# Weight conversions issued behind the first mixed tokens, and three homes for the bias rows' pieces, in a fused attention and MLP-mixer kernel

## The chip, the cores and the metric

The kernel runs on 1 core of a Trainium2 chip, in one launch. The metric is the device time in microseconds (us) of that core. The kernel before was timed in 3 runs: median 874.73 us, lowest 873.62, highest 876.39. The execution whose profile is shown took 872.61 us; from its first to its last instruction (its span) it took 870.8 us.

The engines are called as the profile calls them: PE is TensorE (matmuls), PEld its weight loads, ACT is ScalarE, DVE is VectorE, POOL is GpSimd, SP is SyncE, which only issues DMAs here. A name with a q behind it (SPq, ACTq) is that engine's instruction queue.

## The reference

Four batches of 576 tokens pass through three blocks. All inputs are float32 except the seven weight matrices of the second and third blocks, which lie in memory as 64-bit floats and are converted on the chip.

```python
# attention: q, k, v of 4 batches x 8 heads x 576 tokens x 64
scores = q @ k^T / 8
cum  = cumsum(max(s, 0))                        # per head, along the tokens
bias = -(cum[:, None] - cum[None, :])
scores = where(causal, -1e9, scores + min(bias, 0))
attn = exp(scores - max) / (sum + 1e-9)
x = (attn @ v), heads side by side               # 4 x 576 x 512

# second block: w_k 512x1024, w_v 1024x512, w_r 512x512
x_prev = x shifted by one token
xk = mu_k * x + (1 - mu_k) * x_prev
xr = mu_r * x + (1 - mu_r) * x_prev
v = max(xk @ w_k, 0)^2 @ w_v
x = sigmoid(xr @ w_r) * v

# third block: a mixer over tokens (w_tok1, w_tok2), then over channels (w_ch1, w_ch2)
```

## The kernel before

Nearly all products are made from two parts, a rounded high part and the rest, so that one product costs three matmuls (function `products`, line 108 in the profile). Every weight block is therefore loaded raw and then converted by `weight_split` (lines 614 to 621): two ACT passes over the block, two DVE passes, one ACT pass that writes the high part, and one subtraction that writes the low part (on POOL for w_k and w_r, on DVE for w_v). The blocks of w_k (8) and w_r (4) are 128 x 512 numbers and have five staging buffers; the 16 blocks of w_v are 128 x 256 and are staged in whatever is free of the six buffers named `xt`. At the start four of those hold the attention's output, so that two are left for w_v.

The program starts with batch 0. Its first 256 tokens of all eight heads come first (`early`, lines 324 to 368 of before): scores on PE, maximum on DVE, exponential on ACT, the row sum on POOL, its reciprocal on DVE, the scaling on POOL, a transpose on PE, a copy T on ACT, and a product with V. Behind each transpose PE runs a few matmuls whose result nobody reads (`keep_busy`, line 162). After each pair of heads `mix` (lines 508 to 517) makes one quarter of the mixed tokens HX: two DVE operations, one on ACT (line 516), one on DVE (line 517). Products with w_k that read HX are called h; they need all four quarters for their last terms. The other mixed tokens of the batch are XR; products with w_r that read them are called r; the products with w_v are called vd and need the squared h, KK. The remaining 320 tokens of batch 0's heads (`late`, lines 392 to 421) run between them.

`split_bias` writes the cumulative sums of s, split in two parts, to DRAM (ext_d) in three pieces of 192 columns. Each piece is put together in one tile e: POOL sets it to ones, DVE writes four of its row groups, ACT's queue issues the store (line 202). The tile e has one buffer, so a piece waits for the store of the piece ahead of it. The late heads load ext_d next to their q and k (`late_load`, tiles X).

The order of all instructions on each engine is fixed when the program is built. A scheduler walks through the operations by priority; `with at(place)` gives the place of what stands inside, smaller places first. Each engine then runs its list strictly in order and waits wherever an operand or a buffer is not ready. DMAs from SP and ACT take eight completion counters in turn; each issue waits until the DMA eight places ahead of it has landed.

Of the kernel before, what the change touches and what calls it, by code (L numbers as in the profile page):

```python
# [9 lines left out]
F32R = mybir.dt.float32r  # L10
# [9 lines left out]
def f32(ap):  # L20
    return ap.bitcast(F32)
# [3 lines left out]
def attention_moe_mixer(  # L25
# [16 lines left out]
    nc = tc.nc  # L42
# [25 lines left out]
    def at(place):  # L68
        return tc.high_priority(tc.cur_priority - int(place * 1000))
# [66 lines left out]
    def pt_tile(slot, dtype=F32):  # L136
        return pt_p.tile([128, (NS - 1) * PW], dtype, tag=f"PT{slot}", name=f"PT{slot}")
# [8 lines left out]
    def constants():  # L146
        nc.gpsimd.affine_select(
            out=maskc[:, 512:640], in_=maskc[:, 512:640], pattern=[[-1, 128]],
            compare_op=ALU.is_ge, fill=-8.0e9, base=0, channel_multiplier=1,
        )  # L150
        make_identity(nc, ident)
        nc.gpsimd.memset(maskp, 0.0)
        nc.gpsimd.tensor_copy(maskp[0:TAIL, S // 2 - TAIL:], maskc[0:TAIL, 512:512 + TAIL])
        nc.scalar.dma_start(out=maskp[TAIL:2 * TAIL, S // 2 - TAIL:], in_=maskc[0:TAIL, 512:512 + TAIL])
# [16 lines left out]
    def bias_rows(cp):  # L171
# [14 lines left out]
                copy("D", e32[:, 1, 0, :], cum[:, a:z], -1.0)  # L186
        return cum, e32

    def split_bias(cp, cum, behind):
        n = 3  # L190
        for c in range(n):
            a, z = S * c // n, S * (c + 1) // n
            e = cp.tile([G, 4, 2, z - a], F32R, name="e")
            if c == 0:
                nc.gpsimd.tensor_copy(f32(e[0:1, 0, 1, 0:1]), behind)
            for r, t in ((1, 1), (3, 1), (0, 0), (2, 0)):
                nc.gpsimd.memset(f32(e[:, r, t, :]), 1.0)
            copy("D", e[:, 0, 1, :], cum[:, a:z])
            nc.vector.tensor_tensor(out=e[:, 2, 1, :], in0=cum[:, a:z], in1=f32(e[:, 0, 1, :]), op=ALU.subtract)
            for x in (0, 2):  # L200
                copy("D", e[:, x + 1, 0, :], f32(e[:, x, 1, :]), -1.0)
            nc.scalar.dma_start(out=ext_d[:, :, :, a:z], in_=f32(e))
# [129 lines left out]
    def early(h, j, V0, cp):  # L332
        x, h0, _ = early_view(h)
        w = 128 * j + 128
        P = cp.tile([128, w], F32, tag=f"E{j}", name=f"P{j}", bufs=2)
        mx = st_p.tile([128, 2], F32, tag="mx", name="mx")
        ps = ps_s.tile([128, 512], F32, tag="s", name="s")
        nc.tensor.matmul(ps[:, 0:w], x[0:D + 2, h - h0, 0, 128 * j:w], x[0:D + 2, h - h0, 1, 0:w], start=True, stop=True)
        softmax_max(j, ps, P, mx, 0, 0, w)
        softmax(j, P, mx, 0)  # L340
        if h == 0 and j == 0:
            with at(2):
                split_bias(cp, cum, P[0:1, 0:1])
        if j == 0:
            pt[0] = ps_t.tile([128, 512], F32, tag="t", name="t")
        ps = pt[0]
        for k in range(j + 1):
            o = 128 * (j + k)
            nc.tensor.transpose(ps[:, o:o + 128], P[:, 128 * k:128 * k + 128], ident)
        keep_busy(4, P, 128)  # L350
        if j == 0:
            return
        T = cp.tile([128, FIRST], F32, tag="T", name="T", bufs=2)
        copy("A", T, ps[:, 0:FIRST])
        if h % 2 == 0:
            early_ps[h // 2] = ps_v.tile([128, QC], F32, tag="v", name="pv")
        pv = early_ps[h // 2]
        r = slice(D * (h % 2), D * (h % 2) + D)
        for k in range(2):
            nc.tensor.matmul(pv[r, 128 * k:QC], V0[:, k, h * D:h * D + D], T[:, QC * k:QC + 128 * k], start=k == 0, stop=k == 1)  # L360
        if h % 2 == 1:
            x = xt[0, h // 2] = xt_p.tile([128, 1 + S], F32, tag="xt", name="xt")
            nc.gpsimd.memset(x[:, 0:1], 0.0)
            copy("D", x[:, 1:1 + QC], pv)
# [136 lines left out]
    def mixed(b, c, i):  # L501
# [3 lines left out]
            return act["HX"].rearrange("p (t k s) -> p t k s", t=2, k=KD)  # L505
        return act[("XK", "XR")[i]]

    def mix(b, c, i, p):
        dst = mixed(b, c, i)
        x = xt[b, p]  # L510
        a, z = CHS[c]
        n = z - a
        t = act["mt"].tile([128, act["mtw"]], F32, tag="t", name="t", bufs=act["mtb"])
        nc.vector.tensor_scalar(out=t[:, 0:n], in0=x[:, 1 + a:1 + z], scalar1=mu[:, i, p:p + 1], scalar2=1.0, op0=ALU.mult, op1=ALU.mult)
        nc.vector.scalar_tensor_tensor(out=t[:, 0:n], in0=x[:, a:z], scalar=omu[:, i, p:p + 1], in1=t[:, 0:n], op0=ALU.mult, op1=ALU.add)
        nc.scalar.activation(out=dst[:, 0, p, 0:n], in_=t[:, 0:n], func=AF.Copy)
        nc.vector.tensor_tensor(out=dst[:, 1, p, 0:n], in0=t[:, 0:n], in1=f32(dst[:, 0, p, 0:n]), op=ALU.subtract)  # L517

    def up(b, c, m):
        n = width(c)  # L520
# [84 lines left out]
    def weight_split(key, hi, lo, half=0, ps=None):  # L605
        t = raw.pop(key)
        low, high = t[:, :, :, 0], t[:, :, :, 1]
        if ps is None:
            copy("A", f32(high), f32(high), 2.0 ** -112)
        else:  # L610
            bank = ps.tile([128, high.shape[1], high.shape[2]], I32, tag="w", name="high")
            copy("A", f32(bank), f32(high), 2.0 ** -112)
            high = bank
        nc.scalar.activation(out=low.bitcast(U32), in_=low.bitcast(U32), func=AF.Copy, scale=TOP3, bias=-0.496)  # L614
        nc.vector.scalar_tensor_tensor(out=low, in0=high, scalar=3, in1=low, op0=ALU.logical_shift_left, op1=ALU.bitwise_or)  # L615
        nc.vector.scalar_tensor_tensor(out=low, in0=high, scalar=-2 ** 31, in1=low, op0=ALU.bitwise_and, op1=ALU.bitwise_or)  # L616
        copy("A", hi, f32(low), 0.5 if half else 1.0)
        if half:
            nc.vector.scalar_tensor_tensor(out=lo, in0=f32(low), scalar=0.5, in1=f32(hi), op0=ALU.mult, op1=ALU.subtract)
        else:  # L620
            nc.gpsimd.tensor_tensor(out=lo, in0=f32(low), in1=f32(hi), op=ALU.subtract)  # L621
# [120 lines left out]

    act["mt"], act["mtb"], act["mtw"] = cp, 1, QC
    constants()
    with at(3):
        mixes()
    for h in range(H):
# [15 lines left out]
    for y, a in enumerate(first):  # L763
        nm, W, sw, f = a
        if y:
            with at(x):
                first_load(*a)
        with at(x + 0.6):
            weight_split((nm, f), W[:, 0, :, f:f + 128], W[:, 1, :, f:f + 128], ps=ps_w if nm == "k" else None)
        x += 1.2  # L770
    cp_s.close()
# [12 lines left out]
    for f in range(0, DM, 128):  # L784
        for k in range(0, KF, 2):
            with at(x):
                weight_load((k, f), rows(w_v, k, k + 2)[:, :, f:f + 128], S // 2, xt_p, "xt")
                weight_split((k, f), wv[:, 0, k:k + 2, f:f + 128], wv[:, 1, k:k + 2, f:f + 128], 1)
            x += 1.5
    todo = {}  # L790
    base = (NS - 2) * H
# [232 lines left out]
```

## Time and profile before

| what | us |
|---|---|
| median of 3 runs (lowest, highest) | 874.73 (873.62, 876.39) |
| the profiled execution | 872.61 |
| its span | 870.8 |
| PE busy, of the span | 840.6 |
| DVE busy | 485.1 |
| ACT busy | 452.6 |
| POOL busy | 343.4 |

Busy time counts PE's matmuls that nobody reads as well. Shares over the whole span say little here, since the start, the middle and the end of the program have different limits; the rows further down are therefore cut by stage.

### The profile page before, as it was taken

To read this page: it belongs to the slowest core of one execution; us is meant where nothing else is said; L and a number is where in the kernel's file an instruction comes from. 1 tells how busy PE (TensorE), PEld (TensorE's weight loads), DVE (VectorE), ACT (ScalarE), POOL (GpSimd) and SP (SyncE) were. 2 spreads that over 40 slices of the span, in tenths; PEclk is the share of its full clock that TensorE was granted. 3 is DMA by queue.
4 is the path that set the end of the run, shared out by engine and by line. 5 is a ranking of instruction groups with operands and counts; after the bars stand their busy time and mean duration, and the time that the engine had idled before them with its cause. 6 is when DMAs were issued, how large, how long until landed. Compare 5 with 4: busy or idle time off the path is not lost. (4 is left out here: it accounts for less than half of the span.)

```text
span 870.8 us, 17455 instructions
## 1 busy us (share of the span) xinstructions
PE 840.6 (97%) x6127; PEld 790.5 (91%) x6127; DVE 485.1 (56%) x1352; ACT 452.6 (52%) x1257; POOL 343.4 (39%) x601
## 2 busy tenths in 40 slices
PE   8889998999899999999999999999999999999998
PEld 5656777988789999999999989999999999999998
DVE  5797776565879566985469757951331222222221
ACT  4688766865886656868377865840310221211210
POOL 4565666864785544645256854720000000000000
PEclk9899999999999999999999999999999999999999
DMA  7943778687974244431234746553021112112100
GB/s 191 266 134 88 199 218 230 192 240 210 252 204 133 70 111 117 100 93 41 83 94 129 230 143 217 177 181 94 7 92 54 44 31 74 42 32 73 38 25 26
DMA packets 88024, 108.36 MB, mean 124 GB/s; under 512 B 11152, under 2 KB 71568, under 8 KB 87936
## 3 DMA queue, kind: packets, MB, share of 16 engines
q1 hardware_dynamic: 81408, 91.56, 37.7%
q0 software_dynamic: 4576, 15.08, 5.5%
q8 instruction: 49, 0.80, 0.4%
q10 hardware_dynamic: 1952, 0.60, 0.3%
q14 instruction: 39, 0.32, 0.1%
HBM read 77.74 MB, written 28.90 MB: 122 GB/s over the span
## 5 line engine op out<-in xcount | busy, mean ns | idle before, releaser
L863 ACT ACTIVATE HID<-c 128x256 fp32r<-128x256 f32 (+1 forms) x96 | 39.3, 410 | 220.9 <-PE c L108 220.8
L108 PE MATMUL vd<-KK,WV 128*128 128x256 f32 (+1 forms) x768 | 120.9, 300 | 0.1
L108 PEld LDWEIGHTS vd<-KK,WV 128*128 128x128 f32 x768 | 106.6, 188 | 2.4 <-issue 0.9
L292 POOL TENSOR_SCALAR P<-P,sum 128x128 f32<-128x128 f32 (+4 forms) x148 | 93.6, 636 | 36.2 <-DVE sum L291 30.2
L108 PE MATMUL h<-XK,WK 128*128 128x320 f32 (+1 forms) x672 | 105.9, 303 | 0.7 <-DVE XK L517 0.5
L108 PE MATMUL c<-HID,WV 128*128 128x256 f32 (+1 forms) x768 | 104.9, 291 | 0.0
L108 PE MATMUL c<-U,WK 128*128 128x256 f32 (+1 forms) x768 | 103.2, 291 | 1.4 <-DVE HID L864 1.4
L289 ACT ACTIVATE P<-P,mx 128x128 f32<-128x128 f32 (+4 forms) x148 | 86.9, 588 | 30.3 <-DVE mx L278 23.0
L108 PEld LDWEIGHTS c<-HID,WV 128*128 128x128 f32 x768 | 100.6, 188 | 0.0
L108 PEld LDWEIGHTS c<-U,WK 128*128 128x128 f32 x768 | 98.6, 188 | 1.7 <-DVE HID L864 1.7
L108 PEld LDWEIGHTS h<-XK,WK 128*128 128x128 f32 x672 | 93.8, 189 | 2.1 <-DVE XK L517 0.7
L864 DVE SCALAR_TENSOR_TENSOR HID<-c,HID 128x256 fp32r<-128x256 f32 (+1 forms) x96 | 43.8, 456 | 81.1 <-ACT HID L863 81.0
L278 DVE CUSTOM_DVE_ANT_0 P<-s,maskc 128x128 f32<-128x128 f32 (+4 forms) x148 | 69.1, 478 | 22.1 <-PE t L435 8.4
L928 DVE TENSOR_TENSOR ut<-c,ut 128x256 f32<-128x256 f32 (+1 forms) x32 | 14.6, 458 | 119.3 <-PE c L108 112.0
L529 POOL TENSOR_TENSOR KK<-k,KK 128x256 fp32r<-128x256 f32 (+1 forms) x64 | 55.8, 877 | 19.8 <-ACT k L528 18.7
L108 PE MATMUL r<-XR,WR 128*128 128x320 f32 (+1 forms) x384 | 60.0, 299 | 0.0
L290 POOL TENSOR_SCALAR sum<-sum 128x1 f32<-128x1 f32 (+1 forms) x148 | 32.4, 219 | 67.6 <-ACT P L289 57.2
L108 PE MATMUL c<-HID,WR 128*128 128x256 f32 (+1 forms) x384 | 54.8, 291 | 0.0
L108 PEld LDWEIGHTS r<-XR,WR 128*128 128x128 f32 x384 | 52.8, 188 | 1.1 <-ACT raw L614 0.4
L108 PE MATMUL c<-U,C1A 128*128 128x256 f32 (+1 forms) x384 | 52.8, 296 | 0.1
L108 PEld LDWEIGHTS c<-U,C1A 128*128 128x128 f32 x384 | 51.5, 190 | 0.3 <-ACT U L913 0.3
L108 PEld LDWEIGHTS c<-HID,WR 128*128 128x128 f32 x384 | 51.3, 188 | 0.0
(133 smaller groups left out, 1658.4 us busy)
## 6 DMA issues: line engine op xcount, KB each, us to landing
X<-hl_d SPq DMA_DIRECT2D x72, 288.0 KB
hl_d<-PB SPq DMA_DIRECT2D x48, 288.0 KB
raw<-in_moe_w_ch_dram POOLq DMA_DIRECT2D x48, 256.0 KB, 3.3
PB<-in_qk_dram SPq DMA_DIRECT2D x48, 144.0 KB
yt<-y_d SPq DMA_DIRECT2D x16, 288.0 KB
u_d<-yt SPq DMA_DIRECT2D x16, 288.0 KB
raw<-in_moe_w_k_dram SPq DMA_DIRECT2D x8, 512.0 KB
raw<-in_moe_w_v_dram SPq DMA_DIRECT2D x16, 256.0 KB
```

The lines of the kernel that those rows point to most:

```text
L108: nc.tensor.matmul(ps, a, b, start=first and i == 0, stop=last and i == n - 1)
L278: nc.vector.tensor_tensor_reduce(out=P[0:m, c0:c1], in0=ps[0:m, 0:c1 - c0], in1=mask[0:m], scale=-scale, scalar=3.0e38 if x == 0 else mx[0 ...
L289: nc.scalar.activation(out=P[0:m, 0:w], in_=P[0:m, 0:w], func=AF.Exp, bias=mx[0:m, x:x + 1], scale=-1.0, accum_out=sm[0:m, 0:1])
L290: nc.gpsimd.tensor_scalar(out=sm[0:m, 0:1], in0=sm[0:m, 0:1], scalar1=1e-9, scalar2=1.0, op0=ALU.add, op1=ALU.mult)
L292: nc.gpsimd.tensor_scalar(out=P[0:m, 0:w], in0=P[0:m, 0:w], scalar1=sm[0:m, 1:2], scalar2=1.0, op0=ALU.mult, op1=ALU.mult)
L529: nc.gpsimd.tensor_tensor(out=kk[:, 1, m, 0:n], in0=t[:, 0:n], in1=f32(kk[:, 0, m, 0:n]), op=ALU.subtract)
L863: nc.scalar.activation(out=hi, in_=ps, func=AF.Relu)
L864: nc.vector.scalar_tensor_tensor(out=lo, in0=ps, scalar=0.0, in1=f32(hi), op0=ALU.max, op1=ALU.subtract)
L928: nc.vector.tensor_tensor(out=t, in0=ps, in1=t, op=ALU.add)
```

## The change

There are two edits.

1. `weight_split` of all four blocks of w_r and of the first four blocks of w_v is placed inside `behind_mix()`. It takes the last ACT and the last DVE operation that `mix` has issued so far, which are those of HX's last quarter, and holds the conversions behind them in the order (`tc.issue_after`). Their loads are not held.
2. The three pieces of the bias rows get a tile each: the two PT tiles, which the late heads use afterwards, and e. All ones are set at the program's start (`bias_ones`), and `split_bias` is placed two places earlier (`at(4)` in place of `at(2)`).

```diff
+    def bias_ones(cp, n):
+        for c in range(n):
+            w = S // n
+            e = pt_tile(c, F32R)[0:G, 0:8 * w] if c < 2 else cp.tile([G, 8 * w], F32R, name="e")
+            e = e.rearrange("g (r t s) -> g r t s", r=4, t=2)
+            for r, t in ((1, 1), (3, 1), (0, 0), (2, 0)):
+                nc.gpsimd.memset(f32(e[:, r, t, :]), 1.0)
+            ones.append(e)
+
+    ones = []
+
     def split_bias(cp, cum, behind):
-        n = 3
+        n = len(ones)
         for c in range(n):
             a, z = S * c // n, S * (c + 1) // n
-            e = cp.tile([G, 4, 2, z - a], F32R, name="e")
-            if c == 0:
-                nc.gpsimd.tensor_copy(f32(e[0:1, 0, 1, 0:1]), behind)
-            for r, t in ((1, 1), (3, 1), (0, 0), (2, 0)):
-                nc.gpsimd.memset(f32(e[:, r, t, :]), 1.0)
+            e = ones[c]
+            nc.gpsimd.tensor_copy(f32(e[0:1, 0, 1, 0:1]), behind)
...
-            with at(2):
+            with at(4):
                 split_bias(cp, cum, P[0:1, 0:1])
...
+    last_mix = {}
+
+    def behind_mix():
+        st = ExitStack()
+        for x in last_mix.values():
+            st.enter_context(tc.issue_after(x))
+        return st
...
-        nc.scalar.activation(out=dst[:, 0, p, 0:n], in_=t[:, 0:n], func=AF.Copy)
-        nc.vector.tensor_tensor(out=dst[:, 1, p, 0:n], in0=t[:, 0:n], in1=f32(dst[:, 0, p, 0:n]), op=ALU.subtract)
+        last_mix[0] = nc.scalar.activation(out=dst[:, 0, p, 0:n], in_=t[:, 0:n], func=AF.Copy).ins
+        last_mix[1] = nc.vector.tensor_tensor(out=dst[:, 1, p, 0:n], in0=t[:, 0:n], in1=f32(dst[:, 0, p, 0:n]), op=ALU.subtract).ins
...
+    bias_ones(cp, 3)
...
-        with at(x + 0.6):
+        with at(x + 0.6), behind_mix() if nm == "r" else ExitStack():
             weight_split((nm, f), W[:, 0, :, f:f + 128], W[:, 1, :, f:f + 128], ps=ps_w if nm == "k" else None)
...
-                weight_split((k, f), wv[:, 0, k:k + 2, f:f + 128], wv[:, 1, k:k + 2, f:f + 128], 1)
+                with behind_mix() if x < 18 + 1.5 * 4 else ExitStack():
+                    weight_split((k, f), wv[:, 0, k:k + 2, f:f + 128], wv[:, 1, k:k + 2, f:f + 128], 1)
```

What this makes of the order, at three places. Line numbers move by up to 18 between the two programs. PE, ACT, DVE and SP issue the same operations as before in another order, POOL two more (the copies of one cell); behind about the 1,670th of PE's 5,970 instructions PE's order is the same again.

The first place is ACT's queue around HX's last quarter (P2 to P4 are exponentials of a late head, high and raw conversion passes, WR and WV the passes that write the high parts). Before:

```order
L75 ACTIVATE raw_661<-raw_661 128x512
L614 ACTIVATE raw_661<-raw_661 128x512
L75 ACTIVATE WR_72<-raw_645 128x4x128
L75 ACTIVATE WR_72<-raw_653 128x4x128
L289 ACTIVATE P4_893,sum_901<-P4_893,mx_894 64x576
L75 ACTIVATE WV_71<-raw_700 128x2x128
L75 ACTIVATE PT0_822<-t_823 128x3x128
L516 ACTIVATE HX_368<-t_544 128x256
L75 ACTIVATE WV_71<-raw_708 128x2x128
L75 ACTIVATE PT0_822<-t_860 128x4x128
L289 ACTIVATE P2_946,sum_951<-P2_946,mx_947 128x384
L75 ACTIVATE WR_72<-raw_661 128x4x128
```

And now:

```order
L532 ACTIVATE HX_370<-t_461 128x256
L75 ACTIVATE T_539<-t_515 128x384
L75 ACTIVATE WK_70<-raw_630 128x4x128
L75 ACTIVATE PT0_824<-t_825 128x3x128
L532 ACTIVATE HX_370<-t_546 128x256
L75 ACTIVATE raw_639<-raw_639 128x512
L630 ACTIVATE raw_639<-raw_639 128x512
L75 ACTIVATE raw_647<-raw_647 128x512
L630 ACTIVATE raw_647<-raw_647 128x512
L75 ACTIVATE raw_655<-raw_655 128x512
L630 ACTIVATE raw_655<-raw_655 128x512
L75 ACTIVATE raw_663<-raw_663 128x512
```

Before, 11 of the 12 passes over w_r and 11 of the 12 over w_v's first four blocks stood ahead of HX's last quarter; now all 24 stand behind it. Behind the last row shown come one more pass over w_r, four over w_v's first two blocks, a copy, an exponential, and then the copy of the first h out of PSUM.

The second place is ACT's queue further on, at w_v's third block, raw_702 (raw_700 before). It is loaded into the buffer of the first, and so after that block's last reader, a DVE operation that follows its WV pass. Before, the WV pass of the first block stood here, and the first pass over raw_700 came sixteen rows behind the last of these:

```order
L75 ACTIVATE T_452<-t_428 128x384
L75 ACTIVATE WV_71<-raw_684 128x2x128
L75 ACTIVATE high_621<-raw_619 128x512
L614 ACTIVATE raw_619<-raw_619 128x512
L75 ACTIVATE WV_71<-raw_692 128x2x128
L289 ACTIVATE P1_520,sum_525<-P1_520,mx_521 128x256
```

Now the two stand two rows apart:

```order
L75 ACTIVATE WR_72<-raw_663 128x4x128
L75 ACTIVATE WV_71<-raw_686 128x2x128
L75 ACTIVATE WV_71<-raw_694 128x2x128
L75 ACTIVATE raw_702<-raw_702 128x256
L630 ACTIVATE raw_702<-raw_702 128x256
L75 ACTIVATE raw_710<-raw_710 128x256
L630 ACTIVATE raw_710<-raw_710 128x256
L543 ACTIVATE KK_682<-k_847 128x256
L543 ACTIVATE KK_682<-k_885 128x256
L532 ACTIVATE XR_681<-t_890 128x256
L75 ACTIVATE WV_71<-raw_702 128x2x128
```

Seven rows behind the last of these stands the copy of the third h (k_935), which frees PE's buffer for the fifth.

The third place is SP's queue, behind the fifth block of w_k. Before:

```order
L371 DMA X0_549<-in_qk_dram 64x1152
L597 DMA raw_610<-in_moe_w_k_dram 128x4x256
L371 DMA X1_552<-in_qk_dram 64x1152
L377 DMA VV0_561<-in_v_dram 128x4x128
L378 DMA VV0_561<-in_v_dram 64x128
L377 DMA VV1_564<-in_v_dram 128x4x128
L371 DMA X2_555<-in_qk_dram 64x1152
```

Now:

```order
L379 DMA X0_551<-in_qk_dram 64x1152
L613 DMA raw_612<-in_moe_w_k_dram 128x4x256
L380 DMA X0_551<-ext_d_73 4x1152
L379 DMA X1_554<-in_qk_dram 64x1152
L380 DMA X1_554<-ext_d_73 4x1152
L385 DMA VV0_563<-in_v_dram 128x4x128
L386 DMA VV0_563<-in_v_dram 64x128
L379 DMA X2_557<-in_qk_dram 64x1152
L380 DMA X2_557<-ext_d_73 4x1152
```

The first load from ext_d, which waits for all three stores, now stands third here; before it stood sixteen issues further back. w_k's seventh block moved ahead of the first two loads of w_v.

## Rows read from the trace of the kernel before

**Rows 1.** Busy us (instructions) of each engine by stage; granted clock, DMA share, GB/s
```profile
0.00:14.60 14.60, 11.04 (x53) 6.58 (x53) 6.41 (x28) 4.61 (x13) 6.07 (x28) 1.00 0.66 149
14.60:34.00 19.40, 16.87 (x105) 13.68 (x105) 14.52 (x48) 11.98 (x32) 9.85 (x24) 0.91 1.06 252
34.00:39.00 5.00, 2.92 (x9) 1.90 (x10) 3.17 (x8) 5.00 (x16) 3.88 (x6) 0.65 1.10 315
...
49.10:63.14 14.04, 12.23 (x62) 7.20 (x60) 13.30 (x30) 12.30 (x28) 10.80 (x9) 1.00 0.30 89
63.14:73.21 10.07, 9.80 (x57) 6.55 (x57) 8.65 (x25) 7.83 (x24) 7.45 (x11) 1.00 0.25 82
73.21:91.82 18.61, 18.61 (x106) 12.20 (x105) 14.51 (x45) 16.20 (x51) 9.18 (x16) 1.00 0.41 113
91.82:140.00 48.18, 48.18 (x305) 36.11 (x304) 32.71 (x97) 31.83 (x93) 31.24 (x55) 1.00 0.74 215
140.00:300.00 160.00, 148.63 (x1061) 139.38 (x1060) 113.41 (x368) 117.03 (x330) 107.46 (x199) 0.99 0.72 197
```

**Rows 2.** PE's instructions in order: start, us, what [idle before, releaser]
```profile
49.10 0.48 PE L108 MATMUL h<-HX,WK 128*128 128x256 f32 x2
...
63.14 0.73 PE L108 MATMUL h<-HX,WK 128*128 128x256 f32 x4 [1.21 <-DVE HX L517]
...
73.21 1.66 PE L108 MATMUL h<-HX,WK 128*128 128x256 f32 x12
...
91.82 1.42 PE L108 MATMUL r<-XR,WR 128*128 128x256 f32 x10
...
147.07 0.30 PE L308 MATMUL s<-X 128*128 128x128 f32 x1 [2.31 <-DMA X<-hl_d]
```

**Rows 3.** Waits up to 70 us: us in total, times, longest
```profile
ACT P L289 <- DVE t L514: 4.0, 1, 4.0
...
POOL e L197 <- DMA ext_d<-e: 4.4, 2, 3.4
```

**Rows 4.** ACT's instructions in order
```profile
18.00 0.56 ACTq L202 DMA_DIRECT2D ext_d<-e  x1
...
32.52 0.56 ACTq L202 DMA_DIRECT2D ext_d<-e  x1
33.12 0.40 ACT L289 ACTIVATE P<-P,mx 128x128 f32<-128x128 f32 x1 [4.00 <-DVE t L514]
...
50.52 0.76 ACT L75 ACTIVATE raw<-raw 128x512 f32<-128x512 f32 x1
51.08 0.77 ACT L614 ACTIVATE raw<-raw 128x512 uint32<-128x512 uint32 x1
...
54.16 0.55 ACT L75 ACTIVATE raw<-raw 128x256 f32<-128x256 f32 x1
54.49 0.55 ACT L614 ACTIVATE raw<-raw 128x256 uint32<-128x256 uint32 x1
...
58.63 0.45 ACT L516 ACTIVATE HX<-t 128x256 fp32r<-128x256 f32 x1
```

**Rows 5.** DVE's instructions in order
```profile
27.05 0.25 DVE L77 CAST e<-st 32x192 fp32r<-32x192 f32 x1 [2.02 <-DMA ext_d<-e]
...
62.67 0.41 DVE L517 TENSOR_TENSOR HX<-t,HX 128x256 fp32r<-128x256 f32 x1
```

**Rows 6.** POOL by form, 49 to 64 us: busy, mean ns of one
```profile
L621 POOL TENSOR_TENSOR WR<-raw,WR 128x512 fp32r<-128x512 f32 x3 | 5.8, 1958 | 1.0 <-ACT WR L75 1.0
...
L621 POOL TENSOR_TENSOR WK<-raw,WK 128x512 fp32r<-128x512 f32 x1 | 1.3, 1302 | 1.4 <-DMA raw<-in_moe_w_v_dram 1.4
```

**Rows 7.** SP's issues in order: a pair of w_v's blocks
```profile
79.76 1.15 SPq L597 DMA_DIRECT2D raw<-in_moe_w_v_dram  x2
```

**Rows 8.** ACT's instructions in order, at that pair's first pass
```profile
82.49 0.44 ACT L75 ACTIVATE raw<-raw 128x256 f32<-128x256 f32 x1 [0.41 <-DMA raw<-in_moe_w_v_dram]
```

## The prediction

> **What bounds the kernel now.** I read the table by stage first, then PE's rows in order, then the rows of the engines that PE waits for. The table [rows 1] is to be read for where PE has time that can be won. From 91.8 us on PE is busy nearly throughout: 48.18 of 48.18 us, then 148.63 of 160, and the rest of the span lies in stages that the change does not touch. So a gain can only come from making PE's dense work start earlier. PE's rows show the points to watch [rows 2]: the first h starts at 49.10, the terms of h that need HX's last quarter start at 63.14 (after 1.21 us idle for DVE line 517), the fifth h starts at 73.21 and the first r at 91.82. From 63.14 on PE has no idle time worth naming up to 140 us; a shift of these points is therefore a shift of the end, as long as the same work is done by then and nothing behind eats it.
>
> HX's last quarter is late because ACT and DVE are full at that time: 12.30 and 13.30 of 14.04 us between 49.10 and 63.14 [rows 1]. ACT writes its share at 58.63 [rows 4] and DVE its share at 62.67 [rows 5]. Ahead of it in their queues stand conversions of w_r and w_v, whose products come 28 us later. Before that the bias rows cost two stalls. POOL waits 4.4 us for stores of ext_d, because the three pieces share a tile [rows 3]. ACT stands still for 4.00 us up to the third store's issue at 32.52 and its next exponential at 33.12 [rows 4]; the wait is put down to DVE's t, which was long done, and the issue itself waits for the DMA eight places ahead of it.
>
> **Edit 2, the bias rows.** The pieces no longer wait for each other. The work is the same but for two copies of one cell; the twelve memsets move to the start, where POOL is busy 6.07 of 14.60 us, and DVE's twelve operations fall into its idle time ahead of the first weight block. I cost them at nothing; without that cover it would be about 0.2 us each. What goes is ACT's 4.0 us and POOL's 4.4 us [rows 3], but they don't add up, since w_k's last blocks are late next. DMA is full from 14.6 to 39 (share 1.06 and 1.10 [rows 1]). The core has moved 149 x 14.6 + 252 x 19.4 = 7.06 MB by 34.0 and 8.64 MB by 39.0. In the new order all that SP and ACT issue up to and including w_k's seventh block is 7.5 MB and up to the eighth 8.85 MB (tile shapes of the code: blocks of 0.52, late q and k 0.29 each, stores 0.59, first heads' data 1.6). At the rates of these rows they land at about 35.3 and 39.8. ACT's queue holds the seventh block's pass ahead of head 5's copy and the eighth's ahead of head 6's, so the last heads can't end before.
>
> Behind the eighth block ACT has five passes of 0.57 us over w_k (0.56 from 50.52 to 51.08 [rows 4]), two copies T and one PT, two exponentials of a late head, and two shares of HX: about 5.5 us. HX's last quarter is then done at about 46 instead of 63.0, with a high end of 50 if chains between engines take as long as they did before.
>
> One row speaks against the change here: the second store, issued at 18.00 [rows 4], held DVE until 27.05 [rows 5], 9 us for a small transfer while SP loads w_k. If the second and third store, now issued together near 16, behave like it, they land near 27, and SP stands in front of the load from ext_d until then. The Trainium skill, "DMA: Bandwidth & Descriptors", section "Issuing engines are not separate DMA queues", says that DMAs of different engines run on the same 16 DMA engines and interleave. This wait agrees with it; by it the stores come no sooner for standing on ACT's queue.
>
> That wait on SP is worth little, by rows: 5.7 MB is issued ahead of it, and the core had moved about that much by 27 (7.06 less 7 us at 252 GB/s is 5.3). The low end is nothing, the high end 3 us on HX's last quarter; I take 1, inside the 46.
>
> **Edit 1, the conversions.** ACT loses ahead of HX's last quarter 11 passes over w_r at 0.57 us and 11 over w_v at 0.33 us (54.16 to 54.49 [rows 4]): 9.9 us. All of it returns behind. Between HX's last quarter and the last share of XR, which r needs, ACT had some 19.5 us of work (7.83 and about 12 of the 16.20 us between 63.14 and 91.82 [rows 1]); now it has 29.4. There the order makes a new stall. w_v's third block is loaded into the first's buffer, and its pass stands two rows behind the second block's WV pass. From the issue of a pair at 79.76 [rows 7] to its first pass at 82.49 [rows 8] it took 2.7 us; with the DVE operation ahead of the issue it makes 3.2 us in which ACT stands, and behind it stand KK, XR and, further on, the copy that frees the buffer for PE's fifth h. So ACT's path is 29.4 + 3.2 = 32.6 us if it is never idle otherwise, and at its share of 12.30 / 14.04 = 88% it is 29.4 / 0.88 + 3.2 = 36.6 us. PE needs for the same stretch, from 63.9 to 91.8, 28 us and so waits for ACT. With the high parts of r's first product behind it, r starts between 46 + 32.6 + 1 = 79.6 and 46 + 36.6 + 1.5 = 84.1; I take 84.5, because PE's own queue adds waits for scores' buffers that DVE frees late. The fifth h would start near 67.
>
> By this r comes 91.8 - 84.5 = 7.3 us earlier. PE is then idle twice, some 3 us near 50 and some 4 us near 63. At 34 to 39 PE was busy 2.92 of 5.00 us and its granted clock was 0.65, thus part of the time at 1.2 GHz; behind the idle 2.31 us at 147.07 no such fall is left in the row of that stage (0.99) [rows 1, 2]. The bounds for a fall behind the two gaps are 0 and 3 us (a few us of dense work at half speed); I take 1. POOL's subtractions over w_r took 1958 ns on average with DVE busy beside them, against 1302 ns for the one over w_k [rows 6]; fewer collide now or as many, 0 to 2 us on POOL, which has room.
>
> From 140 us on the waits are for transfers, such as X at 147.07 [rows 2]. The loads that lead to it begin when HX's buffer is free, so they move with PE. I cost a change there at nothing, with 2 us to either side.
>
> **The sum.** -7.3 + 1.0 = -6.3 us; the profiled execution would go from 872.6 to 866.3. It lies 2.1 us below the median of the three runs, so that the median would go from 874.7 to 868.4. I forecast 868.6.
>
> **Rivals.** First, the gain is given back. For it speaks that the moved 9.9 us lie on the engine that PE then waits for, and that 3.2 us of stall are new; against it, that ACT was idle 4.0 us and waited on PE in other places. If HX's last quarter comes at 50 and ACT has the 36.6 us plus 3 of waits on DVE, r starts at 50 + 36.6 + 3 + 1.5 = 91.1: 874, no change.
>
> Second, slower: w_r's and w_v's conversions become what r and vd wait for. Its place is PE's queue at r and the first vd, its price each us by which ACT's queue is later than in the sum; it decides as soon as XR's last share comes after about 90. ACT's and DVE's share would have to fall to 80% (29.4 / 0.80 + 3.2 = 40) with HX at 50 and PE at 1.2 GHz for 3 us: 50 + 40 + 1.5 + 3 = 94.5, thus 877.4. Against it stands that ACT was at 88% where it was the bound.
>
> The clock by itself could do part of that. The Trainium skill, "TensorE: Matmul & The Clock Gate", Part 1, says that the array's clock is gated down to 1.2 GHz when it has been idle and released to 2.4 GHz when it has been busy. The 0.65 at 34 to 39 agrees; by the rule both new gaps would cost something, which the 3 us of the high end hold already.
>
> Third, more gain: the queue runs as in the lower sum, r at 79.6 to 81, and no clock is lost. That is 11 to 12 us, 863.
>
> Fourth, the change does not do what it says, because HX's last quarter is held by w_k's blocks or the stores anyway. With HX at 55 edit 1 has lost most of its sense; the same 872 to 876 as in the first rival come out.
>
> **How the numbers follow.** Forecast (4 to 9 us faster) 0.50; more gain 0.13; given back or without effect 0.22, of which a third still shows 2.6 to 4 us of gain; slower 0.15. About 0.3% (2.6 us) is what a measurement of this kernel can tell from no change. Faster by more: 0.50 + 0.13 + 0.05 = 0.68 with some rounding down of the forecast's edge to 0.67; same 0.18; slower 0.15. The range of 8 in 10 reaches from the third case (862.5) into the slower one (876.5); the likeliest case by itself spans 865.5 to 871.
>
> **What would show it.** ACT's share of HX's last quarter near 45 and DVE's near 46; no wait of POOL or DVE for ext_d and no ACT issue of ext_d behind 20 us; an ACT wait of about 3 us for a load of w_v near 60; the fifth h near 67 and r near 84; PE idle some 7 us between 46 and 67 in place of 2; the stages from 140 us on of the same length. I am wrong if r starts after 89, or if PE's idle time behind 140 us grows by what the start won.

## The result, and the profile after

The changed kernel takes 881.12 us (median of 6 runs, 880.24 to 884.58), the kernel before beside it 874.84 us (6 runs, 871.24 to 876.39). The ratio is 1.0080, with a 95% interval from 1.0058 to 1.0103: slower by 0.8%, where 0.7% faster was forecast, and above the range of 862.5 to 876.5 us. The profiled execution took 880.24 us with a span of 878.5; before it was 872.61 and 870.8.

The first view is the table of stretches of the changed kernel: stretch and length, busy us of PE, PEld, DVE, ACT and POOL with instruction counts, the granted clock of TensorE, the DMA share and GB/s.

```profile
14.00:49.00 35.00, 32.53 (x195) 24.46 (x196) 21.71 (x73) 25.36 (x65) 20.64 (x38) 0.95 1.06 260
49.00:92.00 43.00, 38.87 (x193) 26.01 (x193) 27.11 (x77) 30.89 (x85) 20.26 (x28) 0.84 0.28 78
92.00:140.00 48.00, 47.87 (x298) 35.08 (x297) 39.35 (x108) 34.21 (x100) 30.36 (x49) 1.00 0.72 205
140.00:310.00 170.00, 158.25 (x1116) 147.37 (x1117) 116.97 (x381) 123.23 (x350) 115.64 (x212) 0.98 0.71 193
60.20:67.00 6.80, 6.80 (x27) 5.19 (x26) 3.55 (x10) 4.53 (x12) 6.47 (x8) 0.50 0.05 8
73.90:80.60 6.70, 6.70 (x21) 4.29 (x21) 3.09 (x12) 4.64 (x15) 3.13 (x6) 0.50 0.37 113
```

The same cuts of the kernel before, which [rows 1] has in other cuts:

```profile
14.00:49.00 35.00, 29.49 (x173) 23.77 (x174) 25.73 (x77) 25.64 (x67) 18.74 (x39) 0.85 1.02 260
49.00:92.00 43.00, 40.92 (x224) 26.24 (x223) 36.74 (x98) 36.61 (x102) 27.61 (x36) 1.00 0.34 98
92.00:140.00 48.00, 48.00 (x303) 35.93 (x304) 32.53 (x97) 31.65 (x93) 31.06 (x55) 1.00 0.74 215
140.00:310.00 170.00, 158.63 (x1134) 149.37 (x1133) 120.22 (x385) 124.94 (x349) 113.73 (x207) 0.99 0.69 189
```

PE does the same matmuls in both kernels, so its time can be lost in two ways only: it is idle (length less PE busy), or it runs below full clock (length times what the clock lacks to 1).

| stretch | idle before | idle after | clock before | clock after | difference |
|---|---|---|---|---|---|
| 14 to 49 | 5.5 | 2.5 | 5.3 | 1.8 | -6.5 |
| 49 to 92 | 2.1 | 4.1 | 0.0 | 6.9 | +8.9 |
| 92 to 140 | 0.0 | 0.1 | 0.0 | 0.0 | +0.1 |
| 140 to 310 | 11.4 | 11.8 | 1.7 | 3.4 | +2.1 |

The sum is +4.6 us. It takes the clock from two digits and counts idle time within a slow stretch twice; taken exactly from the trace and without that, the first entry is -6.1 and the sum +5.0. The same matmul stands 5.1 us later in the changed kernel from 302 to 460 us. Another 2.2 us arise between 552 and 578 us, where PE waits once 2.07 us for ACT and the clock is 0.83 from 560 to 570; the code of that stage is the same in both. So the start did win some 6 us. The 43 us behind it gave back 8.9, and 6.9 of those are TensorE at half its clock. Over many executions the clock points the same way: its mean was 0.9915 in 31 executions of the kernel before and 0.9838 in 6 of the changed one. Times the span (one minus the clock) that is 7.4 and 14.2 us, 6.8 us apart, where the medians are 6.3 apart. It is no price that adds up one for one, though: among the executions of the kernel before, in five groups of 21 to 31, one that lost 1 us more to the clock took only 0.3 to 0.5 us longer.

How the clock was lost is seen in PE's rows (start, duration, matmul, in brackets the idle time before it and what ended it):

```profile
53.96 0.71 PE L108 MATMUL h<-HX,WK 128*128 128x256 f32 x4
56.94 1.12 PE L400 MATMUL s<-X 68*128 68x512 f32 x2 [0.35 <-DVE mx L286]
59.74 2.59 PE L108 MATMUL h<-HX,WK 128*128 128x256 f32 x12 [1.68 <-ACT k L542]
63.41 2.93 PE L108 MATMUL h<-HX,WK 128*128 128x256 f32 x12
71.32 0.70 PE L400 MATMUL s<-X 68*64 68x288 f32 x2 [1.38 <-DVE mx L286]
73.14 3.05 PE L400 MATMUL s<-X 68*128 68x384 f32 x4 [0.67 <-DVE mx L286]
```

The last terms of h start at 53.96, 9.2 us earlier than in [rows 2]. Then PE waits 0.35 us for a score's maximum and 1.68 for the first k copy, and later, near 72 us, 1.38 and 0.67 us for maxima, which free its score buffers. Behind each of these two idle places stands a stretch at 0.50, which is 1.2 GHz. An h of twelve matmuls takes 2.59 and 2.93 us there, 1.66 at full clock [rows 2]. The fifth h starts at 75.19 (73.21 before), r at 94.31 (91.82 before).

ACT's rows of the changed kernel show what PE waited for:

```profile
52.07 0.42 ACT L532 ACTIVATE HX<-t 128x256 fp32r<-128x256 f32 x1 [0.40 <-DVE t L531]
52.39 0.67 ACT L75 ACTIVATE raw<-raw 128x512 f32<-128x512 f32 x1
57.93 0.42 ACT L630 ACTIVATE raw<-raw 128x256 uint32<-128x256 uint32 x1
59.33 0.63 ACT L542 ACTIVATE k<-h 128x256 f32<-128x256 f32 x2
68.34 0.44 ACT L75 ACTIVATE raw<-raw 128x256 f32<-128x256 f32 x1 [3.61 <-DMA raw<-in_moe_w_v_dram]
```

From 52.39 to 58.25 twelve passes run on ACT, eight over w_r and four over w_v. The first k copy, which frees the buffer of PE's third h, stands behind them at 59.33, behind a copy and an exponential. At 64.7 ACT stops for 3.61 us for w_v's third block.

### The profile page after: what moved, and what is told of

Same layout as the page of the kernel before. It is cut to its first block, busy times and chain, and to the rows that moved or that the text cites. A ratio compares the mean times of both kernels' runs of the same rounds, so it can differ in the third digit from the quotient of the medians.

```text
span 878.5 us, 17449 instructions
## 1 busy us (share of the span) xinstructions
PE 848.1 (97%) x6127; PEld 794.1 (90%) x6127; DVE 483.2 (55%) x1352; ACT 452.0 (51%) x1257; POOL 341.5 (39%) x603
## 5 line engine op out<-in xcount | busy, mean ns | idle before, releaser
L108 PE MATMUL vd<-KK,WV 128*128 128x256 f32 (+1 forms) x768 | 118.5, 299 | 1.5 <-ACT e L557 1.3
L631 DVE SCALAR_TENSOR_TENSOR raw<-raw 128x256 int32<-128x256 int32 (+2 forms) x77 | 40.6, 529 | 25.0 <-ACT raw L630 17.1
```

The lines of the kernel that those rows point to most:

```text
L108: nc.tensor.matmul(ps, a, b, start=first and i == 0, stop=last and i == n - 1)
```

## The experiments

Two theories were put against each other. Theory A: the held conversions stand ahead of the first k copies in ACT's list, PE falls idle, the clock falls, and that eats the gain. Theory B: the new homes of the bias rows cost the time. From the fifth run on theory C stood beside them: any change upstream makes the planner lay out a new order, and the order of the kernel before is a good one among many. Each kernel ran beside the kernel before on the same chip (medians of that 874.5 to 875.6 us). The clock is the mean over a kernel's executions; the last two columns are PE's idle time and its time lost to the clock from 49 to 92 us, from the table of stretches of one profiled execution, which may lie off the median (e6's took 871.8 us, e11's 891.3, e12's 875.7, e17's 875.0). The mean clock does not order the times by itself: e5 takes 879.0 us at 0.9916, e13 875.3 at 0.9866.

| run | us | ratio, 95% interval | clock | idle | half clock |
|---|---|---|---|---|---|
| before | 874.7 | | 0.9915 | 2.1 | 0.0 |
| after | 881.1 | 1.0080, 1.0058 to 1.0103 | 0.9838 | 4.1 | 6.9 |
| e1 homes only | 877.3 | 1.0026, 1.0006 to 1.0047 | 0.9855 | 4.2 | 3.4 |
| e2 holding only | 889.8 | 1.0159, 1.0131 to 1.0186 | 0.9808 | 4.0 | 6.9 |
| e3 w_r held | 881.6 | 1.0077, 1.0050 to 1.0104 | 0.9845 | 2.7 | 3.4 |
| e4 w_v held | 874.8 | 0.9999, 0.9986 to 1.0013 | 0.9887 | 3.4 | 3.4 |
| e5 before, a copy | 879.0 | 1.0048, 1.0030 to 1.0066 | 0.9916 | 2.1 | 1.7 |
| e6 before, 8 copies | 874.8 | 1.0003, 0.9981 to 1.0024 | 0.9881 | 2.7 | 0.0 |
| e7 after, PE busier | 884.6 | 1.0114, 1.0090 to 1.0138 | 0.9865 | 3.3 | 3.4 |
| e8 w_v held, PE busier | 881.4 | 1.0081, 1.0062 to 1.0101 | 0.9867 | 2.7 | 3.4 |
| e9 before, a copy | 876.2 | 1.0018, 1.0002 to 1.0034 | 0.9877 | 1.2 | 1.7 |
| e10 before, a copy | 876.1 | 1.0015, 0.9997 to 1.0032 | 0.9878 | 2.1 | 0.0 |
| e11 after, a copy | 881.8 | 1.0081, 1.0052 to 1.0111 | 0.9810 | 4.6 | 10.8 |
| e12 after, a copy | 879.5 | 1.0044, 1.0025 to 1.0063 | 0.9868 | 5.7 | 5.2 |
| e13 after, w_r passes out | 875.3 | 0.9998, 0.9985 to 1.0012 | 0.9866 | 4.1 | 3.4 |
| e14 before, w_r passes out | 882.8 | 1.0080, 1.0055 to 1.0104 | 0.9832 | 5.9 | 6.9 |
| e15 after, pass on POOL | 878.8 | 1.0032, 1.0018 to 1.0046 | 0.9860 | 2.4 | 3.4 |
| e16 w_v held, early busier | 882.0 | 1.0067, 1.0044 to 1.0090 | 0.9871 | 3.0 | 6.9 |
| e17 one w_r block held | 880.3 | 1.0049, 1.0026 to 1.0072 | 0.9893 | 3.1 | 0.0 |
| e18 two w_r blocks held | 874.8 | 0.9998, 0.9979 to 1.0016 | 0.9917 | 2.9 | 0.0 |

**The parts alone.** e1 leaves both holds out of the changed kernel, e3 the one of w_v, e4 the one of w_r; e2 has the old `split_bias` with both holds.

```diff
-        with at(x + 0.6), behind_mix() if nm == "r" else ExitStack():        # e1, e4
+        with at(x + 0.6), ExitStack():
-                with behind_mix() if x < 18 + 1.5 * 4 else ExitStack():      # e1, e3
+                with ExitStack():
```

> The bias rows' pieces in three homes, as in the changed kernel; no conversion is held back. Theory A (the held conversions cost the time: in ACT's in-order queue they stand ahead of the first k copies, PE falls idle, and the 1.2 GHz that follows eats what was won): the stalls on the bias rows are gone, HX's last quarter comes 2 to 5 us before the 62.7 us it has in the kernel before, no stage behind it is at 1.2 GHz, 870 to 874 us. Theory B (the new homes and their later issue cost the time, the held conversions don't): 878 to 883 us, with the loss already there at 55 us.

> The conversions of w_r's blocks and of w_v's first four held behind the mixed tokens, as in the changed kernel; the bias rows as in the kernel before, with their stalls on the shared tile. Theory A: 878 to 886 us, with a stretch of 5 us or more at a granted clock near 0.5 between 55 and 85 us, as in the changed kernel (0.50 from 60 to 67 and from 74 to 81). Theory B: 866 to 872 us, no such stretch.

> The changed kernel with w_r's conversions alone held; w_v's run early again. Theory A with the conversions ahead of the k copies as its main part: 8 of the 12 passes that stood between HX's last quarter and the first k copy remain, the first low-clock stretch stays, the second (behind the wait for w_v's third block) goes: 873 to 879 us. If the wait of 3.61 us for w_v's third block is the main part: below 874 us. Theory B: 878 to 883 us.

> The changed kernel with the conversions of w_v's first four blocks alone held; w_r's run early again. The wait for w_v's third block stays, and 4 of the 12 passes ahead of the k copies. If the wait for that block is the main part of the loss: 877 to 883 us, one stretch at a clock near 0.5 about 10 us behind HX's last quarter. If the passes ahead of the k copies are the main part: 871 to 876 us. Theory B: 878 to 883 us.

Theory B falls with e2: with the old homes the loss is 15 us, not none. But e1 is not the gain that theory A gave it either: it has a stretch at 1.2 GHz without any held conversion, and HX's last quarter is no earlier (DVE's share starts at 63.22 us, 62.67 in the kernel before). e3 lost its second slow stretch, as theory A said, but was above its range. Holding w_v costs nothing to be measured: e4 is level with the kernel before and 2.5 us below e1, but ACT does not wait for a block of w_v ahead of r there, against 3.61 us in the changed kernel, so that e4 doesn't price that wait. Holding w_r is slower by 4.3 us without w_v (e3 against e1) and by 6.3 with it (the changed kernel against e4). Of e2's loss, which is more than theory A allowed, 8.5 us arise between 227 and 304 us by the shift of its matmuls; what makes them there was not followed up. Its HX was the earliest of all (DVE's last share starts at 50.50) and its r among the latest (98.82): an early HX alone is worth nothing.

e1's rows show another way into the same trap. First DVE, then POOL, then PE:

```profile
58.84 1.01 DVE L631 SCALAR_TENSOR_TENSOR raw<-raw 128x512 int32<-128x512 int32 x2
59.78 2.12 DVE L632 SCALAR_TENSOR_TENSOR raw<-raw 128x512 int32<-128x512 int32 x2
61.82 0.68 DVE L286 CUSTOM_DVE_ANT_0 P<-s,maskc 128x512 f32<-128x512 f32 x1
```

```profile
59.73 1.29 POOL L637 TENSOR_TENSOR WR<-raw,WR 128x512 fp32r<-128x512 f32 x1 [0.76 <-ACT WR L75]
```

```profile
62.56 1.65 PE L400 MATMUL s<-X 68*128 68x384 f32 x2 [2.95 <-DVE mx L286]
```

Here the conversions' DVE passes stand in a bunch ahead of a score's maximum, which frees PE's score buffer, and PE is idle for 2.95 us in one piece.

**A useless copy.** e5, e9 and e10 do one k copy of the kernel before twice, 0.36 us more on ACT; e6 does eight more of the first; e11 and e12 do one twice in the changed kernel.

```diff
+        for _ in range(1 if (b, c, m) == (0, 0, 0) else 0):     # e6: 8; e9: m 2; e10, e12: m 4; e11: m 0
+            nc.scalar.activation(out=t[:, 0:n], in_=ps, func=AF.Relu)
         nc.scalar.activation(out=t[:, 0:n], in_=ps, func=AF.Relu)
```

> The kernel before, with the first k copy of the first h done twice on ACT: 0.36 us more work, everything else as written; the planner lays the order out anew behind it. It says how much a change without a purpose moves this kernel. Theory A (the loss of the changed kernel is PE at 1.2 GHz behind idle stretches that the held conversions made): within 3 us of the kernel before, 872 to 878 us. Theory C (any change of the order costs this much, because the order of the kernel before is a lucky one): 878 to 884 us, with the loss spread over 140 to 300 us.

> The kernel before, with the first k copy of the first h done nine times on ACT: 8 x 0.36 = 2.9 us more ahead of the buffer that PE's third h needs, nothing else moved by hand. Theory A: PE is idle 2 us or more near 62 to 66 us, the granted clock falls to about 0.5 behind it for several us, and the kernel takes more than the 2.9 us longer: 878 to 884 us. Rival (idle time alone costs): 874 to 878 us, clock at 1.00 in 49 to 92 us.

> The kernel before with the k copy of the third h done twice: 0.36 us more on ACT, and a new order behind it from the planner. Theory C (the order behind the change decides, and that of the kernel before is a good one among many): 876 to 882 us, like the 879.0 us of the kernel with the first copy done twice. Theory A (the held conversions themselves cost the time; such a control is neutral on average): 872 to 876 us.

> The kernel before with the k copy of the fifth h done twice: 0.36 us more on ACT, a new order behind it. Theory C: 876 to 882 us. Theory A: 872 to 876 us.

> The changed kernel with the k copy of the first h done twice: 0.36 us more on ACT, a new order behind it. Theory A: 879 to 885 us, the loss of the changed kernel stays whatever the order behind it, with 5 us or more at half clock between 55 and 92 us. Theory C: anything from 874 to 885 us; a time below 877 us would speak for it.

> The changed kernel with the k copy of the fifth h done twice: 0.36 us more on ACT, a new order behind it. Theory A: 879 to 885 us. Theory C: anything from 874 to 885 us; a time below 877 us would speak for it.

One copy of 0.36 us cost 4.3 us in e5 and some 1.6 in e9 and e10 (e10's interval still holds no difference), and eight copies (2.9 us) cost nothing in e6. PE has more of the list ahead of its first r there (462 recorded matmuls, 446 in the kernel before); from 49 to 92 us it is idle for 2.7 us in all, and in the profiled execution, which was 3 us faster than the median, the clock stays at 1.00. Theory A's expectation for e6 was wrong and its rival's came true; e11 and e12 fit both A and C. Theory C is shown in part: five orders of the kernel before have medians from 874.7 to 879.0 us, 876.2 on average, and the one that is timed as before is, with e6, the lowest of them. The three orders of the changed kernel lie at 879.5, 881.1 and 881.8, 880.8 on average. By these few orders, of the 6.3 us about 1.5 are the luck of the order compared with, and about 4.6 stay with the change. That is an estimate: with the versions below that do less work on ACT counted in, the averages are 877.3 (e14) and 879.3 us (e13, e15), 2.0 apart.

**More for PE to do.** e7 and e8 have the unread matmuls also behind late head 1's transposes, in the changed kernel and in e4; e16 has five in place of four behind each early transpose, in e4.

```diff
-        if h < 1 and m == 128:            # e7, e8
+        if h < 2 and m == 128:
-        keep_busy(4, P, 128)              # e16
+        keep_busy(5, P, 128)
```

> The changed kernel, with the six unread matmuls on P that late head 0 has after its transposes also after those of head 1: some 1.5 us more work for PE near 69 to 73 us, where it stood idle 1.38 and 0.67 us. Theory A: the second stretch at 0.50 (73.8 to 80.7 us) gets shorter or goes, and the kernel is faster for having more to do: 876 to 880 us. Rival (the waits cost, the clock follows them but decides nothing): 881 to 884 us.

> Three homes, only w_v's first four blocks held, and the six unread matmuls also behind head 1's transposes. Theory A: the stretch at 0.52 near 58 to 65 us gets shorter or goes: 870 to 874 us, less than the kernel before. Rival (the waits cost): 875 to 878 us.

> Three homes, only w_v's first four blocks held, and five in place of four unread matmuls behind each early head's transposes, to keep PE busy while it waits for w_k (the stretch at half clock near 34 us). Theory A: less time at half clock before 49 us, but the conversions are where they were: 872 to 876 us, at best 2 us below the kernel before. Rival (PE's extra work counts): 876 to 880 us.

All three are slower than the kernels they start from, by 3.5, 6.6 and 7.2 us. e7 did lose less to the clock from 49 to 92 us (3.4 for 6.9), but lost more ahead of 49 (8.4 for 4.3, idle time and clock) and from 140 to 310. As a test of the clock they are worth little, because each also made a new order; as versions they are refuted.

**Taking the passes away.** e13 and e14 leave out ACT's two passes over w_r, in the changed kernel and in the one before; e15 has the first of them on POOL.

```diff
-        if ps is None:
+        skip = key[0] == "r"              # e13, e14; hi and lo are then made from high
+        if skip:
+            pass
+        elif ps is None:
             copy("A", f32(high), f32(high), 2.0 ** -112)
...
-            copy("A", f32(high), f32(high), 2.0 ** -112)
+            copy("P" if key[0] == "r" else "A", f32(high), f32(high), 2.0 ** -112)   # e15
```

> The changed kernel without ACT's two passes over each of w_r's four blocks (8 passes of 0.57 us; WR's high parts are then taken from the raw words, so r is another number; DVE's passes stay). Theory A (the loss is PE's clock behind the idle time that the held passes make on ACT ahead of the k copies): PE waits 1 us or less for the k copy ahead of its third h, no stretch at 0.50 between 55 and 70 us, mean granted clock 0.988 or more in place of 0.984, 871 to 876 us. Rival (the loss comes from elsewhere in the start, or from the order behind it): 878 to 883 us, clock 0.984.

> The kernel before without the same 8 passes, as the control for the one above: what 4.6 us less work on ACT is worth by itself. Theory A: 871 to 876 us, within 3 us of the changed kernel without them. Rival: 868 to 873 us, the same distance below the changed kernel without them as with them.

> The changed kernel with the first of the two passes over each w_r block on POOL, which was busy 3.6 of 14 us there, in place of ACT. 8 in place of 12 passes stand ahead of the first k copy on ACT. Theory A: k copy some 2 us earlier, less time at half clock, 875 to 880 us. Rival: 880 to 884 us.

e13 comes out at 875.3 us, in theory A's range, and the wait for the k copy is gone; but for the wrong reason, since PE waits longer than before, in another place. Its rows on DVE, POOL and PE:

```profile
53.93 5.81 DVE L635 SCALAR_TENSOR_TENSOR raw<-raw 128x512 int32<-128x512 int32 x4
59.66 0.55 DVE L286 CUSTOM_DVE_ANT_0 P<-s,maskc 128x384 f32<-128x384 f32 x1
```

```profile
54.22 6.68 POOL L643 TENSOR_TENSOR WR<-raw,WR 128x512 fp32r<-128x512 f32 x4 [4.02 <-ACT WR L75]
```

```profile
60.27 1.22 PE L400 MATMUL s<-X 68*64 68x288 f32 x2 [4.08 <-DVE mx L286]
```

Four DVE passes over w_r and four POOL subtractions run beside each other and hold the score's maximum for 5.8 us. e15 came out in theory A's range too: the k copy starts 4.6 us behind DVE's share of HX in place of 6.8, half as much is lost to the clock from 49 to 92 us, and it is still slower than the kernel before. And e14 is the surprise: 4.6 us less work on ACT makes the kernel before 7 us slower. Its table from 49 to 92 us has 5.9 us of idle PE and a clock of 0.84, and its waits are of the same kind:

```profile
49.00:92.00 43.00, 37.15 (x187) 24.21 (x187) 31.52 (x85) 28.25 (x82) 24.71 (x31) 0.84 0.30 89
```

```profile
55.38 1.24 PE L392 MATMUL s<-X 68*128 68x384 f32 x2 [1.13 <-DVE mx L278]
60.86 1.22 PE L392 MATMUL s<-X 68*64 68x288 f32 x2 [1.93 <-DVE mx L278]
63.78 0.90 PE L401 MATMUL t<-ident,P 128*128 128x128 f32 x3 [1.70 <-POOL P L292]
```

So the loss needs no held conversions, and it does not need more work on ACT.

**One or two of w_r's blocks.** If the number of bunched passes set the loss, holding one and two blocks would lie between e4 (none) and the changed kernel (four).

```diff
-        with at(x + 0.6), behind_mix() if nm == "r" else ExitStack():
+        with at(x + 0.6), behind_mix() if nm == "r" and f >= 384 else ExitStack():   # e17; e18: f >= 256
```

> The changed kernel with only the last of w_r's four blocks held (w_v's four as in the change). Between holding none of w_r (874.8 us) and all (881.1 us). Theory A (each pass that is bunched behind the mixed tokens costs): 875 to 878 us, PE's waits and half clock between 49 and 92 us between those of the two. If the plan behind decides alone: anything from 874 to 884 us, without an order by the number of blocks.

> The changed kernel with the last two of w_r's four blocks held (w_v's four as in the change). Theory A: 876 to 880 us, above the kernel that holds one and below the one that holds four. If the plan behind decides alone: anything from 874 to 884 us, without an order by the number of blocks.

They do not: none 874.8, one 880.3, two 874.8, four 881.1. Both lie outside what theory A gave them, and theory A in this form is refuted. e18's row shows that w_r held by half can pass without any loss to the clock:

```profile
49.00:92.00 43.00, 40.13 (x238) 27.39 (x237) 31.42 (x85) 36.04 (x100) 24.05 (x36) 1.00 0.35 96
```

What is shown: where the changed kernel's time went (PE's idle time and its clock, 49 to 92 us above all); that both holds together, or w_r's alone, are slower than the kernel before in every order tried with the same passes (seven medians from 878.8 to 889.8 us; e13, which leaves passes out, is level with it); that the homes with at most half of w_r held, and no unread matmuls added, lie between 874.8 and 880.3; and that none of the 18 kernels is measurably faster than the kernel before. What stays open: which feature of a new order makes the long wait. It was the k copy in the changed kernel and in e3, the score's maximum in e1, e4, e13 and e14, and POOL's scaling in e2 (2.79 us). The part of the 4.6 us that comes from all of w_r being held, and not from the orders that this happens to give, could not be told apart further.

## Why the prediction was wrong, step by step

| step | predicted | measured |
|---|---|---|
| bias rows' stalls | both go, stores issued near 16 | gone; issued at 13.53, 14.91 and 16.16 |
| SP held by the stores | in the adverse case to 27 us | loads behind them issued at 22.10, some 2.7 us of waiting |
| w_k's seventh and eighth block | 35.3, 39.8 | first passes at 37.03, 42.36 |
| HX's last quarter done | 46, high end 50 | 52.9 |
| ACT's new wait on w_v | 3.2 us near 60 | 3.61 us up to 68.34 |
| fifth h | 67 | 75.19 |
| r | 84.5 | 94.31 |
| PE idle near 50 and 63 | 3 and 4 us | 0.35 and 1.68 near 58, 2.05 near 72 |
| clock behind it | 1 us, 0 to 3 | 6.9 us |

Edit 2 took the stalls away as the prediction said, but by e1 it does not bring HX forward by itself. w_k's last two blocks were 1.7 and 2.6 us later than worked out, and HX's last quarter 7 us. 3.1 us of that is a step that was given only as the high end, "if chains between engines take as long as they did before". PE's rows of the changed kernel show the chain:

```profile
45.92 1.16 PE L162 MATMUL idle<-P 128*128 128x128 f32 x8
47.01 0.70 PE L400 MATMUL s<-X 68*64 68x288 f32 x2
47.64 1.34 PE L108 MATMUL h<-HX,WK 128*128 128x256 f32 x9
48.81 1.05 PE L162 MATMUL idle<-P 128*128 128x128 f32 x8
49.80 0.87 PE L368 MATMUL pv<-T,V 128*64 128x256 f32 x4
```

The copy T that the last pv needs was written by 46.7, but PE's list has unread matmuls, a score and the first terms of h ahead of it, so that pv starts at 49.80. DVE waits 3.9 us for it, and ACT as long for the transposes behind it. An engine's own list counts as a wait, also where the engine is busy.

The step that failed is r's start, 84.5 us predicted and 94.31 measured; the prediction's own sign of being wrong, r after 89, came true. 6.9 of the 9.8 us are HX's last quarter. The rest is the path behind it. The prediction went from HX to r along ACT's list and let PE wait for ACT. It sized that list about right: from DVE's share of HX, done at 52.94, to ACT's last share of XR, done at 88.84, it took 35.9 us for the 32.6 to 36.6 worked out. But r does not wait for it. DVE's share of XR is ready at 90.22, and PE, which runs without a wait worth naming from 73.14 on, comes to r 4.1 us later:

```profile
89.82 0.40 DVE L533 TENSOR_TENSOR XR<-t,XR 128x256 fp32r<-128x256 f32 x1
94.31 1.65 PE L108 MATMUL r<-XR,WR 128*128 128x256 f32 x12
```

In the kernel before it was the same: XR was ready at 85.62, and the row of r at 91.82 in [rows 2] has no wait.

```profile
85.20 0.42 DVE L517 TENSOR_TENSOR XR<-t,XR 128x256 fp32r<-128x256 f32 x1
```

Nor does PE wait ahead of its first r in any of the 18 other kernels. What sets r is PE's own list: the work in it, the idle time and the clock. Ahead of r that list is the same but for four transposes (450 recorded matmuls for 446), some 76 us at full clock in both; the rest of the 94.31 is 9.6 us of idle time and 8.5 of clock. For r at 84.5 only some 8 us would be left for the two, 3.0 of which pass idle ahead of 14 us, while the prediction counts 8 from 46 us on. The sum could have shown it: it gave r 7.3 us while it let PE's idle time grow by 5 and added 1 for the clock, so that 13.3 us would have to go elsewhere. Counted in idle time and clock, the kernel before has 5.5 + 5.3 + 2.1 = 12.9 us to be won between 14 and 140 us, 10.8 of them ahead of 49. The yardstick itself, "a shift of these points is therefore a shift of the end, as long as the same work is done by then", held up to 140 us: r is 2.5 us later, and the table's sum up to there is 2.5. In e13 it did not hold: r starts at 85.65, 6.2 us earlier than in the kernel before, with 429 recorded matmuls ahead of it and 4.9 us more lost from 140 to 310 us, and that kernel takes 875.3 us.

The second failure is a size: the clock term, taken as 1 us with bounds of 0 to 3, is 6.9. The low bound was read from 147.07 in [rows 2], where 2.31 us of idle time left the stage at 0.99; a hundredth of 160 us is 1.6 us, and the prediction called that nothing; cut finer, the clock is 0.91 from 140 to 160 us. The high bound counted one fall of a few us for two gaps. The Trainium skill, "TensorE: Matmul & The Clock Gate", Part 1, says that the clock is gated when the array has been idle, and the changed kernel's two stretches at 0.50 agree; what the rule did to the time had to come from the rows.

The third is a term that is missing: a new order by the planner, worth 0 to 4 us by the controls. The rival that ended slower gave 877.4 us with r at 94.5; r came at 94.31. But that is luck: its mechanism was w_r's and w_v's conversions as what r waits for, with 3 us at 1.2 GHz, and r did not wait for them, though XR's last share did come at about the 90 us that it named. ACT waited for PE instead, from 78.9 to 82.31 us, for 3.38. From 140 to 310 us the kernel lost 2.1 us more, at the edge of the 2 us that were allowed, and the stage near 560 added 2 more. One sum of the chances is off, too: a third of 0.22 is 0.07 and not 0.05.

## What to carry to other kernels

Where one engine is the bound, write down its idle time and its clock loss by stage first: that is all there is to win, and each microsecond of a forecast must come off one of those entries. Where a planner lays out the order afresh at each edit, run two or three edits without a purpose before believing a difference of half a per cent; this kernel sat at the good end of its own scatter. Before a product's start is taken as a yardstick, look whether it waits at all: where it doesn't, only less work, idle time or clock loss ahead of it in its engine's list moves it. Work that is moved off a critical chain in one bunch can make a long wait elsewhere, as here, though e18 shows that it need not; such a wait can cost more through the clock than by its length.

## What the hardware showed that was not expected

Two waits of PE in short order, 0.35 and 1.68 us, then 1.38 and 0.67, each pair with some 1.1 us of work between, were followed both times by a stretch of some 6.8 us at 1.2 GHz in which PE had work throughout (6.80 of 6.80 us busy). They cost 6.9 us, the waits themselves 4.1. Waits of such a size did not always have this consequence: in e17 PE waited 0.91, 0.41 and 1.40 us between 53.7 and 58.9 us, and the clock was 1.00 from 49 to 92.

DVE's passes over 512 columns took 0.68 us alone and 1.45 on average (5.81 for four) in e13 while POOL subtracted, and POOL's four took 1.67 each in place of 1.30. One by one, DVE's first pass, which began ahead of POOL, took 0.68 us and the other three 1.77 to 1.80, and the two engines ended in turn: POOL at 55.79, DVE at 56.34, POOL at 57.50, DVE at 58.04, POOL at 59.19, DVE at 59.74. The Trainium skill, "SBUF — State Buffer", section "SBUF: two separate sides", says that DVE and GpSimd lock a shared pair of ports against each other for whole instructions when a DVE operation has two inputs in SBUF and the GpSimd operation reads SBUF, as both do here; these rows agree, since both engines slow down and end in turn. On this kernel it matters because the held passes are of just this kind, and a score's maximum queues behind them.
